# Scaled keys turned to token order by VectorE and SBUF transfers in place of TensorE, in a gated linear attention kernel followed by a feed-forward layer

## The chip, the core and the metric

The kernel runs as one program on one core of a Trainium2 chip. The metric is the device time of one execution in microseconds. The core's engines run side by side, each working through its own queue in order: TensorE (PE, with its weight loads shown apart as PEld), VectorE (DVE), ScalarE (ACT), GpSimd (POOL) and SyncE (SP), which here issues all transfers between device memory and the on-chip memory SBUF, and inside SBUF. Matmul results land in PSUM, which this kernel uses as eight banks.

## The reference

`state` is a 48 by 48 matrix for each of 4 batches and 8 heads. For each of 768 tokens it is decayed row by row by `alpha`, receives the outer product of `k` and `v`, and is read by `q`. The result, 3072 tokens by 384, goes through two matrix products with a leaky ReLU between them.

```python
for t in range(S):
    state = alpha[:, :, t, :, None] * state + np.einsum('bhd,bhe->bhde', k[:, :, t], v[:, :, t])
    y[:, :, t] = np.einsum('bhd,bhde->bhe', q[:, :, t], state)
...
h = x @ w_in
g = np.maximum(0.01 * h, h)
return (g @ w_out).astype(np.float32)
```

## The kernel before

The tokens are cut into 24 **units** of 128 tokens: unit u is token block u // 4 of batch u % 4, all 8 heads of it. Three units make one of eight **groups** of 384 tokens for the feed-forward layer.

The attention of a unit goes in eight steps (`attention`): `scans` (cumulative products of alpha, forward and backward), `scores` (keys times queries, line 356), `mask_scores`, `k_tokens`, `scaled_q`, `scaled_k`, `outputs` and `next_state`. The scans, `scaled_q` and `scaled_k` of unit u+1 stand between the steps of unit u. Keys and queries are scaled with the cumulative products in a layout with the head's 48 entries on the partitions and the tokens along the row (`ks`, `qs`: 128 partitions, 4 head pairs of 128 tokens each). `scores` uses that layout. The update of the state (line 412) needs the scaled keys the other way round, tokens on the partitions; `k_tokens` makes that: four TensorE transposes into a PSUM bank (line 380) and one ScalarE copy into SBUF (`ktok`, line 382). Units 20 to 23 are the last token blocks and update no state, so they skip it.

Alpha, q and k of units 0 to 8 are loaded token by token and turned by TensorE (line 280). From unit 9 on (`AHEAD`), they are loaded by four transfers each (line 146) in such a shape that one VectorE transpose in 32 by 32 blocks (line 289) gives the layout above. The transfers of these units write into fixed rooms in SBUF, two for each of alpha, q and k (`NL`), used in turn; units 0 to 8 have a third room each (`spare`). `load_next(u, i)` asks for the next load as soon as the room has been read.

The feed-forward layer is cut into **items** (i, f): group i, slice f of 16 of the hidden width. One item is 9 matmuls into a bank `ph` (line 493, two such banks), a ScalarE multiply and a VectorE maximum that free the bank (`t`, lines 496 and 499), a ScalarE rounding (`gh`, 501), a VectorE remainder (`gl`, 505), and, three items later in the code, 9 matmuls into the three output banks of the group (line 520). After 16 items, ScalarE copies the three outputs (`o`, line 532, two buffers) and SP sends them out (line 534). Groups 0 and 1 run alternately while the weights are converted; groups 2 to 7 run one after the other, and beside them the attention of units 9 to 23, one unit ahead of what the next group needs (`SL`, `LEAD`). `gather` (line 449) moves part of a group's attention output inside SBUF with two transfers before the group's first item.

The order of the instructions on each engine is not the order of the code: the tile framework schedules the whole program with its own estimate of times, and from there on the order is fixed. Groups 2 to 7 use three PSUM banks `a` for the attention in rotation (scores two, key transposes one, outputs one, state update one), three `b` for group outputs, two `ph`.

## Time and profile before

| | |
|---|---|
| median of 3 timed runs | 532.39 us (529.51 to 532.51) |
| span of the profiled execution | 530.9 us |
| TensorE busy, matmuls / weight loads | 518.5 us / 500.0 us |
| VectorE busy | 379.0 us |
| ScalarE busy | 230.7 us |
| GpSimd busy | 62.6 us |
| DMA queue of SP, share of 16 engines | 39.5% |

The profile gives the span from the first to the last instruction, not a separate time for that execution; the span lies between the lowest and the median of the timed runs. A line of a group of instructions reads: source line, engine, operation, output and inputs by name, count, then total busy time and the mean of one in nanoseconds, then the idle time of the engine just before them and who ended it. A line of the timeline reads: start and duration in us, engine, line, operation, names, count, and in brackets the idle time before it with what ended it. In the trace each single-precision matmul of lines 356, 395, 401 and 412 shows as two weight loads and two matmuls; the transposes of line 380 show as one each.

### The profile page before, as it was taken

The numbers are of one execution on the slowest core, as the hardware profiler recorded it, in microseconds if no ns is written. First come the engines' busy times: TensorE is split into PE (matmuls) and PEld (weight loads), VectorE is DVE, ScalarE is ACT, GpSimd is POOL, SyncE is SP. The second block draws the span as 40 slices with busy tenths as digits, with TensorE's granted clock in tenths as the row PEclk, the third lists the DMA queues.
The fourth block names the chain that finished last, engine by engine and source line by source line (L and its number), as shares of the span: only waits on it lengthen the run. The fifth ranks groups of instructions, "written<-read, shape, count | busy, mean of one in ns | idle before, by whom it ended". The sixth has DMA issues, their size and how long they took to land.

```text
span 530.9 us, 9962 instructions
## 1 busy us (share of the span) xinstructions
PE 518.5 (98%) x3778; PEld 500.0 (94%) x3778; DVE 379.0 (71%) x695; ACT 230.7 (43%) x489; POOL 62.6 (12%) x143
## 2 busy tenths in 40 slices
PE   8997999999999999999999999999999999999995
PEld 7886999999999999999999999999999999999995
DVE  6998899999999997777577586585786534333331
ACT  2764855555534444444334444345344444333331
POOL 4554500000000111100101101101010000000000
PEclk9998999999999999999999999999999999999998
DMA  9999975545726533552251431433201000101001
GB/s 144 168 175 170 229 172 133 131 122 141 170 45 184 127 84 81 102 134 49 60 111 30 112 83 44 92 74 86 54 15 25 31 16 1 23 1 44 1 0 51
DMA packets 92982, 46.64 MB, mean 88 GB/s; under 512 B 57856, under 2 KB 90112, under 8 KB 92928
## 3 DMA queue, kind: packets, MB, share of 16 engines
q1 hardware_dynamic: 92928, 45.93, 39.5%
q8 instruction: 32, 0.52, 0.4%
q14 instruction: 22, 0.18, 0.1%
HBM read 38.83 MB, written 4.72 MB: 82 GB/s over the span
## 4 chain that ended last, share of the span: by engine, by line
PE 87%; DVE 7%; DMA 4%; issue 1%; SPq 0%; DVEq 0%; ACT 0%
PE ph L493 35%; PE b L520 32%; PE a L356 4%; PE a L401 3%; PE a L520 3%; DMA small<-in_v_dram 3%; PE a L395 3%; PE a L412 2%; PE b L401 1%; PE a L380 1%; PE b L280 1%; DMA small<-in_alpha_dram 1%; DVE pw L262 1%; DVE gl L505 1%; DVE t L499 1%
## 5 line engine op out<-in xcount | busy, mean ns | idle before, releaser
L493 PE MATMUL ph<-large,w 128*128 128x384 f32 x1152 | 226.6, 338 | 0.5 <-DVE t L499 0.5
L493 PEld LDWEIGHTS ph<-large,w 128*128 128x128 f32 x1152 | 200.1, 188 | 2.8 <-DVE t L499 1.1
L520 PE MATMUL b<-w,gh 128*128 128x384 f32 x672 | 168.9, 340 | 0.0
L499 DVE TENSOR_TENSOR t<-ph,t 128x384 f32<-128x384 f32 x128 | 70.7, 553 | 79.1 <-ACT t L496 78.9
L520 PEld LDWEIGHTS b<-w,gh 128*128 128x128 f32 x672 | 119.4, 188 | 2.1 <-issue 0.4
L496 ACT ACTIVATE t<-ph 128x384 f32<-128x384 f32 x128 | 62.5, 489 | 128.2 <-PE ph L493 128.2
L501 ACT CAST gh<-t 128x384 fp32r<-128x384 f32 x128 | 65.7, 513 | 119.6 <-DVE t L499 119.6
L520 PE MATMUL b<-w,gl 128*128 128x384 f32 x336 | 107.4, 335 | 0.0
L505 DVE TENSOR_TENSOR gl<-t,gh 128x384 fp32r<-128x384 f32 x128 | 70.9, 554 | 34.3 <-ACT gh L501 34.2
L520 PEld LDWEIGHTS b<-w,gl 128*128 128x128 f32 x336 | 62.6, 188 | 0.0
L367 POOL TENSOR_SCALAR_AFFINE_SELECT sm<-sm 128x512 f32<-128x512 f32 x33 | 23.1, 712 | 207.8 <-ACT sm L366 207.8
L356 PEld LDWEIGHTS a<-qs,ks 48*128 48x128 f32 x312 | 24.1, 188 | 5.1 <-issue 4.2
L356 PE MATMUL a<-qs,ks 48*128 48x128 f32 x312 | 28.7, 285 | 0.0
L289 DVE STREAM_TRANSPOSE ks<-small 128x512 f32<-128x512 f32 x15 | 16.7, 1123 | 14.6 <-PE a L380 14.6
L324 POOL COPY pe<-pc 128x4 f32<-128x4 f32 x24 | 4.8, 202 | 163.7 <-DVE pc L314 163.7
L373 POOL TENSOR_TENSOR small<-us,pe 48x192 f32<-48x192 f32 x40 | 22.4, 560 | 1.5
L314 DVE TENSOR_TENSOR_SCAN pc<-e,small 128x128 f32<-128x128 f32 x60 | 20.4, 401 | 0.0
L366 ACT COPY sm<-a 128x512 f32<-128x512 f32 x24 | 14.0, 583 | 14.0 <-PE b L356 12.9
L520 PE MATMUL a<-w,gh 128*128 128x384 f32 x96 | 19.6, 337 | 0.0
L320 DVE TENSOR_TENSOR_SCAN rc<-e,small 128x511 f32<-128x511 f32 x15 | 19.1, 1276 | 0.2
L401 PE MATMUL a<-sm,small 128*48 128x128 f32 x256 | 17.7, 277 | 0.0
L254 ACT CAST w<-bits 128x768 fp32r<-128x768 f32 x16 | 13.4, 838 | 8.4 <-DVE bits L251 7.8
(92 smaller groups left out, 554.4 us busy)
## 6 DMA issues: line engine op xcount, KB each, us to landing
raw<-in_moe_w_out_dram SPq DMA_DIRECT2D x16, 384.0 KB, 3.8
small<-in_v_dram SPq DMA_DIRECT2D x24, 192.0 KB, 3.7
raw<-in_moe_w_in_dram SPq DMA_DIRECT2D x32, 144.0 KB, 4.0
out_dram<-o SPq DMA_DIRECT2D x24, 192.0 KB, 2.0
small<-in_alpha_dram SPq DMA_DIRECT2D x32, 96.0 KB, 2.3
small<-in_q_dram SPq DMA_DIRECT2D x30, 96.0 KB, 2.4
small<-in_k_dram SPq DMA_DIRECT2D x30, 96.0 KB, 2.2
small<-in_alpha_dram SPq DMA_DIRECT2D x30, 80.0 KB, 2.4
```

The lines of the kernel that those rows point to most:

```text
L314: nc.vector.tensor_tensor_scan(pc[:, p, :], aT[:, p, :], ones.broadcast_to([P, C]), 1.0, ALU.mult, ALU.mult)
L320: nc.vector.tensor_tensor_scan(flat[2][:, NP * C - 2::-1], flat[0][:, NP * C - 1:0:-1], flat[1][:, NP * C - 2::-1], last, ALU.mult, ALU.add)
L356: nc.tensor.matmul(ss[s][:, p, :], ks[lo:lo + D, p, :], qs[lo:lo + D, p, :], start=True, stop=True)
L367: made["mask", u] = nc.gpsimd.affine_select(out=sm[s], in_=sm[s], compare_op=ALU.is_ge, fill=0.0, base=0, pattern=[[0, NP], [1, C]], chann ...
L373: nc.gpsimd.tensor_tensor(*scalings.pop(0))
L401: nc.tensor.matmul(y[lo:lo + m, p, :], V[:, c:c + m], masked[u][s][:, p, :], start=not tb and p == 0, stop=p == NP - 1, skip_group_check=True,
L493: nc.tensor.matmul(ph, w_in_of(f, wn, g), xt[:, g, :], start=n == 0, stop=n == 3 * NG - 1)
L496: put(ordered, "ACT", lambda: nc.scalar.mul(t, ph, 0.01))
L499: put(ordered, "DVE", lambda: nc.vector.tensor_tensor(t, ph, t, ALU.max))
L501: put(ordered, "ACT", lambda: nc.scalar.copy(gh, t))
L505: made["gl", i, f] = put(ordered, "DVE", lambda: nc.vector.tensor_tensor(gl, t, gh.bitcast(F32), ALU.subtract))
L520: product = nc.tensor.matmul(po[j], gt[:, js], w_out_of(f, wn), start=f == 0 and n == 0, stop=f == NF - 1 and n == 2)
```

## The change

For units 9 to 19 the keys are no longer turned by TensorE and copied by ScalarE. After `scaled_k`, the new `turn_keys` lets VectorE transpose the scaled keys in 32 by 32 blocks (a second transpose for the unit, written into the room that the unit's k was loaded to), and 16 transfers inside SBUF, 32 partitions of 512 or 256 bytes each, put the blocks where they belong in the room that the unit's q was loaded to. The state update reads the keys from there. Within a token the four head pairs now alternate, so that the weights of one state-update matmul lie four elements apart. The next load of k waits until the 16 transfers have read, the next load of q until the state update has read. Alpha and k of units 9 to 23 have one room each in place of two; units 0 to 8 keep three. Units 0 to 8 keep the TensorE transposes.

```diff
--- before.py
+++ after.py
@@ -49,7 +49,8 @@
     ps_h = fast.enter_context(tc.tile_pool(name="ps_h", bufs=2, space=bass.MemoryType.PSUM))
     ps_x = fast.enter_context(tc.tile_pool(name="ps_x", bufs=3, space=bass.MemoryType.PSUM))
 
-    NL = 2, 2, 2
+    NL = 1, 2, 1
+    NS = 2, 1, 2
     NV = 3
     NBITS, NPW, NRAW = 2, 1, 4
     T4 = 4
@@ -89,7 +90,8 @@
     state, vals_sb, rest = rest[:B], rest[B:B + NV], rest[B + NV:]
     loads_sb = [[rest.pop(0) for _ in range(n)] for n in NL]
 
-    spare = pieces("spare", F32, *[(NP * PITCH,)] * 3)
+    spare = pieces("spare", F32, *[(NP * PITCH,)] * sum(NS))
+    spare_sb = [[spare.pop(0) for _ in range(n)] for n in NS]
     x_sb, = pieces("large", F32R, (3 * (NG + 1), 2, TB))
 
     w_sb = {}
@@ -110,7 +112,7 @@
         return tc.issue_after(made[key].ins) if key in made else nullcontext()
 
     def places(u, i):
-        return loads_sb[i] + [spare[i]] if u < AHEAD else loads_sb[i]
+        return loads_sb[i] + spare_sb[i] if u < AHEAD else loads_sb[i]
 
     def loaded(u, i):
         return places(u, i)[u % len(places(u, i))]
@@ -334,7 +336,8 @@
     def scaled_q(u):
         pc = live[u][0]
         qT = transposed(u, 1, "qs")
-        load_next(u, 1)
+        if not turns(u):
+            load_next(u, 1)
         qs = qT if u >= AHEAD else atp.tile([P, NP, C], F32, name="qs")
         nc.vector.tensor_tensor(qs, qT, pc, ALU.mult)
         live[u].append(qs)
@@ -342,10 +345,14 @@
     def scaled_k(u):
         pc, rc, pe, qs = live[u]
         kT = transposed(u, 2, "ks")
-        load_next(u, 2)
+        if not turns(u):
+            load_next(u, 2)
         ks = kT if u >= AHEAD else atp.tile([P, NP, C], F32, name="ks")
         made["ks", u] = nc.vector.tensor_tensor(ks, kT, rc, ALU.mult)
         live[u] = [pe, qs, ks]
+        if turns(u):
+            turn_keys(u, ks)
+            load_next(u, 2)
 
     def scores(u):
 
@@ -372,8 +379,30 @@
             while scalings:
                 nc.gpsimd.tensor_tensor(*scalings.pop(0))
 
+    turned = {}
+
+    def turns(u):
+        return u >= AHEAD and units[u][0] < NC - 1
+
+    def turn_keys(u, ks):
+
+        Q = 32
+        kq, ktok = (loaded(u, i)[:, 0:NP * C] for i in (2, 1))
+        nc.vector.transpose(
+            kq.rearrange("r (c e p) -> r p c e", c=C // Q, p=NP), ks.rearrange("r p (c t) -> r p c t", t=Q)
+        )
+        for r in range(0, P, Q):
+            n = min(Q, BR - r) * NP
+            for c in range(C // Q):
+                nc.sync.dma_start(
+                    ktok[c * Q:(c + 1) * Q, r * NP:r * NP + n], kq[r:r + Q, c * Q * NP:c * Q * NP + n]
+                )
+        turned[u] = ktok.rearrange("t (e p) -> t p e", p=NP)
+
     def k_tokens(u):
-        if units[u][0] < NC - 1:
+        if u in turned:
+            live[u][2] = turned.pop(u)
+        elif units[u][0] < NC - 1:
             ks = live[u][2]
             kt = bank()
             for p in range(NP):
@@ -413,6 +442,8 @@
                         kv[lo:lo + m, p, :], ktok[:, p, lo:lo + m], V[:, h * D:(h + 1) * D], start=True, stop=True
                     )
         load_values(u + NV)
+        if turns(u):
+            load_next(u, 1)
         live[u] = pe, kv
         xh, xl = (x_sb[0:BR, at:at + NP, n, j * C:(j + 1) * C] for n in (0, 1))
         made["xh", u] = nc.scalar.copy(xh, y[0:BR])
```

All line numbers above 52 shift. In the rows of the changed kernel below, 291 stands for 289 (VectorE transposes of loads), 316, 318 and 322 for 314, 316 and 320 (scans), 342 and 351 for 339 and 347 (scaling of q and k), 363 for 356, 371 for 364, 424 for 395, 430 for 401, 441 for 412, 450 for 419, 467 for 436, 524 for 493, 530 for 499, 536 for 505, 551 for 520; on SP 148 for 146 and 160 for 158. New are 391 (the VectorE transpose of scaled keys) and 397 (the 16 transfers).

**First place: TensorE where unit 9 begins**, in group 2. The names `w_801`, `w_1035` and so on are the weight slices of the items. Before:

```order
L493 MATMUL ph<-large,w_1017 128x384 x9
L520 MATMUL b<-w_801,gh 128x384 x5
L356 MATMUL a<-qs,ks 128x128 x8
L380 MATMUL a<-small,ks 128x112 x4
L493 MATMUL ph<-large,w_1035 128x384 x9
L520 MATMUL b<-w_801,gl 128x384 x2
L520 MATMUL b<-w_801,gh 128x384
L520 MATMUL b<-w_801,gl 128x384
L493 MATMUL ph<-large,w_1103 128x384 x7
L395 MATMUL a<-qs,small 112x128 x4
```

Now (`w_1254` is slice 7, `w_1329` slice 8, `w_1101` slice 5; before, `w_1017` was slice 3):

```order
L524 MATMUL ph<-large,w_1254 128x384 x6
L363 MATMUL a<-qs,ks 128x128 x8
L524 MATMUL ph<-large,w_1254 128x384 x2
L424 MATMUL a<-qs,small 112x128 x4
L524 MATMUL ph<-large,w_1254 128x384
L524 MATMUL ph<-large,w_1329 128x384 x9
L551 MATMUL b<-w_1101,gh 128x384 x2
L551 MATMUL b<-w_1101,gl 128x384
L441 MATMUL a<-small 64x48
L441 MATMUL a<-small 48x48
L441 MATMUL a<-small 64x48
L441 MATMUL a<-small 48x48
```

The four transposes of line 380 are gone. The scores of unit 9 have moved from behind slice 3 to inside slice 7, and the attention's matmuls, which stood in two blocks, stand in more and shorter ones, with feed-forward matmuls between them.

**Second place: the start of group 3.** TensorE before (`w_1616` and `w_1679` are slices 12 and 13 of group 2, `w_667` is slice 0 of group 3):

```order
L520 MATMUL b<-w_1616,gh 128x384 x2
L520 MATMUL b<-w_1616,gl 128x384
L493 MATMUL ph<-large,w_667 128x384 x9
L520 MATMUL b<-w_1679,gh 128x384 x2
L520 MATMUL b<-w_1679,gl 128x384
L520 MATMUL b<-w_1679,gh 128x384 x2
L520 MATMUL b<-w_1679,gl 128x384
L520 MATMUL b<-w_1679,gh 128x384 x2
L520 MATMUL b<-w_1679,gl 128x384
L395 MATMUL a<-qs,small 112x128 x4
L401 MATMUL a<-sm,small 48x128 x8
```

TensorE now (`w_1795` is slice 15 of group 2, `w_665` and `w_799` are slices 0 and 1 of group 3):

```order
L551 MATMUL b<-w_1795,gh 128x384 x2
L441 MATMUL a<-small 64x48
L551 MATMUL b<-w_1795,gl 128x384
L551 MATMUL b<-w_1795,gh 128x384 x2
L551 MATMUL b<-w_1795,gl 128x384
L551 MATMUL b<-w_1795,gh 128x384
L430 MATMUL a<-sm,small 48x128 x8
L551 MATMUL b<-w_1795,gh 128x384
L551 MATMUL b<-w_1795,gl 128x384
L524 MATMUL ph<-large,w_665 128x384 x9
L524 MATMUL ph<-large,w_799 128x384 x4
L441 MATMUL a<-small 48x48
```

Before, group 3 began while slices 13, 14 and 15 of group 2 still had their second products to come. Now all second products of group 2 stand ahead of it.

VectorE before, from the key transpose of unit 14 to slice 0 of group 3 (the second `t`) and on:

```order
L289 STREAM_TRANSPOSE ks<-small 128x4x4x32
L499 TENSOR_TENSOR t<-ph,t 128x384
L314 SCALAR_TENSOR_TENSOR pc<-e,small 128x128 x4
L315 MEMSET e 128x32
L316 RECIPROCAL small<-pc 128x32
L505 TENSOR_TENSOR gl<-t,gh 128x384
L320 SCALAR_TENSOR_TENSOR rc<-e,small 128x511
L499 TENSOR_TENSOR t<-ph,t 128x384
L347 TENSOR_TENSOR ks<-ks,rc 128x512
L289 STREAM_TRANSPOSE e<-small 128x4x4x32
L505 TENSOR_TENSOR gl<-t,gh 128x384
L289 STREAM_TRANSPOSE qs<-small 128x4x4x32
```

VectorE now, from the last step of unit 11's group (line 450) over the key transpose of unit 13 and slice 0 of group 3 (the first `t`) to slice 1 (the second `t`) and on:

```order
L450 TENSOR_TENSOR large<-a,large 112x4x128
L291 STREAM_TRANSPOSE ks<-small 128x4x4x32
L530 TENSOR_TENSOR t<-ph,t 128x384
L351 TENSOR_TENSOR ks<-ks,rc 128x512
L467 TENSOR_TENSOR us<-small,a 48x192 x2
L291 STREAM_TRANSPOSE qs<-small 128x4x4x32
L536 TENSOR_TENSOR gl<-t,gh 128x384
L391 STREAM_TRANSPOSE small<-ks 128x4x128
L530 TENSOR_TENSOR t<-ph,t 128x384
L342 TENSOR_TENSOR qs<-qs,pc 128x512
L291 STREAM_TRANSPOSE e<-small 128x4x4x32
L530 TENSOR_TENSOR t<-ph,t 128x384
```

Before, the key transpose of a unit stood more than one slice ahead of slice 0. Now that of unit 13 stands right ahead of slice 0's maximum, and the new transpose (line 391) ahead of slice 1's.

**Third place: SP's queue over one unit.** Before, the loads of k, alpha, q and v of one unit:

```order
L146 DMA small<-in_k_dram 32x4x192 x2
L146 DMA small<-in_k_dram 32x4x160 x2
L146 DMA small<-in_alpha_dram 32x4x192 x2
L146 DMA small<-in_alpha_dram 32x4x160 x2
L146 DMA small<-in_q_dram 32x4x192 x2
L146 DMA small<-in_q_dram 32x4x160 x2
L158 DMA small<-in_v_dram 128x8x48
```

Now, with the 16 transfers of unit 13 among them:

```order
L148 DMA small<-in_q_dram 32x4x192 x2
L148 DMA small<-in_q_dram 32x4x160
L397 DMA small<-small 32x128 x12
L397 DMA small<-small 32x64 x4
L148 DMA small<-in_k_dram 32x4x192 x2
L148 DMA small<-in_k_dram 32x4x160 x2
L148 DMA small<-in_q_dram 32x4x160
L565 DMA out_dram<-o 128x384
L148 DMA small<-in_alpha_dram 32x4x192 x2
L148 DMA small<-in_alpha_dram 32x4x160 x2
L160 DMA small<-in_v_dram 128x8x48
```

The 16 transfers stand behind most of the next load of q and ahead of the next loads of k and alpha. Before, no load of this stretch stood behind a transfer inside SBUF other than a gather.

## The prediction, made before the changed kernel was run

> **What bounds the kernel now.** I read the busy times and the chain of waits first, because they say which engine a saved microsecond must lie on:
>
> ```profile
> PE 518.5 (98%) x3778; PEld 500.0 (94%) x3778; DVE 379.0 (71%) x695; ACT 230.7 (43%) x489; POOL 62.6 (12%) x143
> ...
> PE 87%; DVE 7%; DMA 4%; issue 1%; SPq 0%; DVEq 0%; ACT 0%
> ```
>
> TensorE (PE) is busy for 98% of the span and makes 87% of the chain. Next I asked for busy times in two stretches of the stage in which units 9 to 19 run (columns: stretch, its length, then PE, PEld, DVE, ACT, POOL with counts, granted clock, DMA share, GB/s):
>
> ```profile
> 180.00:210.00 30.00, 30.00 (x215) 29.00 (x215) 24.80 (x48) 12.42 (x29) 4.23 (x10) 1.00 0.38 87
> 360.00:390.00 30.00, 30.00 (x219) 29.04 (x218) 20.82 (x40) 13.10 (x30) 4.11 (x10) 1.00 0.20 52
> ```
>
> PE is busy for all of both, at a granted clock of 1.00. VectorE has 5.2 us of 30 free in the first and 9.2 in the second. So in this stage time goes only with what PE has to issue, and comes only where PE is made to wait. Since a busy PE may hold several matmuls in flight, I price PE's work by the distance from one block's start to the next in the timeline (start, duration, idle before in brackets), not by durations. The pace of the units, from the scores of two units nine apart:
>
> ```profile
> 201.10 0.97 PEld L356 LDWEIGHTS a<-qs,ks 48*128 48x128 f32 x16 [0.25 <-issue]
> 383.22 0.97 PEld L356 LDWEIGHTS a<-qs,ks 48*128 48x128 f32 x16 [0.25 <-issue]
> ```
>
> 182.1 / 9 = 20.2 us a unit.
>
> **The transposes that go.** The groups of line 380 in the stage, and where the first and one other of them stand on PE:
>
> ```profile
> L380 PE MATMUL a<-small,ks x44: 257/258/314, 173.6 to 367.9; 112*128 112x112 f32 x44
> ...
> 172.51 0.97 PEld L356 LDWEIGHTS a<-qs,ks 48*128 48x128 f32 x16 [0.25 <-issue]
> 173.60 0.39 PEld L380 LDWEIGHTS a<-small,ks 112*128 112x128 f32 x4
> 173.94 1.51 PEld L493 LDWEIGHTS ph<-large,w 128*128 128x128 f32 x9
> ...
> 222.03 0.51 PEld L380 LDWEIGHTS a<-small,ks 112*128 112x128 f32 x4
> 222.50 0.30 PEld L520 LDWEIGHTS b<-w,gh 128*128 128x128 f32 x2
> ```
>
> 44 transposes, four a unit. The first four move what follows by 0.34 us (173.94 − 173.60), standing right behind the scores. The other ten sets stand alone, and each costs 0.47 (222.50 − 222.03). The two weight loads after it take 0.30 where such a pair elsewhere takes 0.36 (254.25, quoted below), so about 0.05 is given back. Sum: 10 × (0.47 − 0.05) + 0.34 = **4.5 us off PE**. One transpose lasts 258 ns, but four start within 0.47: they overlap, and 44 × 0.258 = 11.4 would count the same time twice. [...] ScalarE's copies of line 382 go with them; ScalarE is busy 12 to 13 us of 30 above, and no row has PE waiting for those copies: 0.
>
> **The new blocks.** The attention's single-precision matmuls stand between feed-forward ones, and each change between them costs something:
>
> ```profile
> 249.73 0.83 PEld L401 LDWEIGHTS a<-sm,small 128*48 128x48 f32 x16
> 250.53 0.59 PEld L412 LDWEIGHTS a<-small,ktok 128*64 128x64 f32 x16
> 251.18 0.30 PEld L520 LDWEIGHTS b<-w,gh 128*128 128x128 f32 x2
> ...
> 252.69 1.57 PEld L493 LDWEIGHTS ph<-large,w 128*128 128x128 f32 x9
> 254.25 0.36 PEld L520 LDWEIGHTS b<-w,gh 128*128 128x128 f32 x2
> ...
> 255.82 0.36 PEld L493 LDWEIGHTS ph<-large,w 128*128 128x128 f32 x2
> ...
> 414.24 1.01 PEld L395 LDWEIGHTS a<-qs,small 112*112 112x112 f32 x8
> 415.38 0.82 PEld L401 LDWEIGHTS a<-sm,small 128*48 128x48 f32 x16
> 416.39 1.52 PEld L493 LDWEIGHTS ph<-large,w 128*128 128x128 f32 x9 [0.18 <-PE a L401]
> 417.89 0.19 PEld L520 LDWEIGHTS b<-w,gh 128*128 128x128 f32 x1
> ```
>
> Line 401 followed by line 412 takes 0.80 to the next start; followed by the feed-forward layer it takes 1.01, and the nine loads behind that take 1.50 in place of 1.56. So one change costs 0.21 less 0.06, about 0.16 to the rounding of the rows. Behind line 412 it costs nothing that can be seen (0.65, then 0.30), and ahead of the scores 0.25 (201.10). In PE's order for units 9 to 19 I count 41 single-precision blocks before, ten of them transposes alone, and 47 now. That is 47 − 31 = 16 more, at 0 to 0.25 each: 0 to 4.0. I take the nearest row, 0.16: **+2.6**.
>
> **Weights four elements apart.** Line 412 (now 441) reads its weights with a step of 16 bytes. No matmul of before loads weights with a step, so I bound it. The 16 loads of a unit take 0.65 us to the next start (251.18 − 250.53), 0.041 each:
>
> ```profile
> L412 PEld LDWEIGHTS a<-small,ktok 128*64 128x64 f32 (+1 forms) x304 | 12.8, 134 | 0.7 <-ACT pc L332 0.5 <-issue 0.2
> ...
> L289 DVE STREAM_TRANSPOSE ks<-small 128x512 f32<-128x512 f32 x15 | 16.7, 1123 | 14.6 <-PE a L380 14.6
> ...
> L347 DVE TENSOR_TENSOR ks<-ks,rc 128x512 f32<-128x512 f32 x15 | 10.3, 686 | 0.0
> ```
>
> Lower end: 0, since one load lasts 134 ns while the next starts after 41, so a slower read may hide in the overlap. Upper end: a block that takes twice as long, 11 × 0.65 = 7.2. A gain is out, as the same numbers are read. The nearest row with a step is VectorE's transpose, which writes four elements apart and takes 1123 ns for 512 elements where a plain product takes 686; but it does another operation. The blocks are now shorter, one to four matmuls between feed-forward loads in several units, so some of the extra lies beside other work. I stay nearer the lower end: **+2.0**. [...]
>
> **VectorE.** The new transpose moves as many elements as that of line 289: 11 × 1.12 = 12.3 us. That is 1.1 in each 20.2 us, against 5.2 and 9.2 free in 30: it is covered by PE. If it stands right ahead of a `t` (line 499, which frees the bank that PE wants) the cover is thin. An old case of that:
>
> ```profile
> 161.09 2.04 DVE L289 STREAM_TRANSPOSE ks<-small 128x512 f32<-128x512 f32 x2
> 162.95 0.57 DVE L499 TENSOR_TENSOR t<-ph,t 128x384 f32<-128x384 f32 x1
> ...
> 163.57 1.53 PEld L493 LDWEIGHTS ph<-large,w 128*128 128x128 f32 x9 [0.79 <-DVE t L499]
> ```
>
> Two transposes ahead of `t` made PE idle for 0.79. In the new order the second no longer stands there: **−0.8**.
>
> **The transfers and the start of group 3.** Rows for what the new wait consists of:
>
> ```profile
> 263.74 1.74 SPq L146 DMA_DIRECT2D small<-in_k_dram  x4
> ...
> L449 SPq DMA_DIRECT2D large<-large x16: 568/584/1405, 39.1 to 451.8; - x16
> ...
> small<-in_k_dram SPq DMA_DIRECT2D x30, 80.0 KB, 2.3
> ...
> large<-large SPq DMA_DIRECT2D x16, 144.0 KB, 4.0
> ...
> L493 PE MATMUL ph<-large,w 128*128 128x384 f32 x1152 | 226.6, 338 | 0.5 <-DVE t L499 0.5
> ...
> L499 DVE TENSOR_TENSOR t<-ph,t 128x384 f32<-128x384 f32 x128 | 70.7, 553 | 79.1 <-ACT t L496 78.9
> ...
> L496 ACT ACTIVATE t<-ph 128x384 f32<-128x384 f32 x128 | 62.5, 489 | 128.2 <-PE ph L493 128.2
> ...
> L505 DVE TENSOR_TENSOR gl<-t,gh 128x384 fp32r<-128x384 f32 x128 | 70.9, 554 | 34.3 <-ACT gh L501 34.2
> ...
> L436 DVE TENSOR_TENSOR us<-small,a 48x192 f32<-48x192 f32 x22 | 7.6, 347 | 0.3
> ```
>
> SP's queue takes 0.435 us for one load of k (1.74 / 4) and 0.584 for a transfer inside SBUF of another shape; these land 2.3 and 4.0 us later. The 16 transfers so take 7.0 to 9.3 us to issue and 2.3 to 4.0 for the last to land. With one room, the last of the next four loads of k (0.43, landing 2.3; the others go out while the transfers land) waits for them, VectorE's key transpose (1.12) waits for that load, and everything behind it in VectorE's queue waits too. Where that transpose is ahead of a `t`, PE waits in the end.
>
> This decides at group 3. Slice 0's `t` there stands right behind the key transpose of unit 13. From the end of the first product of slice 13 of group 2, VectorE reaches the end of unit 12's new transpose after PE's tail 0.3 (0.338 for one matmul of line 493), `t` 0.49 + 0.55, key scaling 0.69, query transpose 1.10, two `us` 0.69, `gl` 0.55 and the transpose 1.12: 5.5 us. The chain from there to slice 0's `t` is issues, landing, 0.43 + 2.3 + 1.12 + 0.55: 13.7 to 17.7, middle 15.7. So slice 0's bank is free 19.2 to 23.2 us later. PE must have it for slice 2. Until then its order holds four first products and six second products at 1.57 (255.82 − 254.25), and the attention blocks (scores 1.09 + 0.25, line 395's 1.14, 401's 0.80, nearly two of 412's, 1.2): 20.2. It waits 1.0 (0 to 3.0). Slice 1's `t` stands behind the rest of unit 13 on VectorE: 0.69 + 0.69 + 1.12 + 0.55 + 1.12 + 0.55 = 4.7 later, while PE has 1.57 + 1.05 of work: 2.1 more. Second products would fill that, but all of group 2's have been issued ahead. **+3.1** (2.1 to 5.1, and 0 where the chain is faster than its lower end). At the later group starts second products of the old group still stand behind slice 0, as they did before: 0.
>
> **Sum.** −4.5 − 0.8 + 2.6 + 2.0 + 3.1 = +2.4. The profiled execution has a span of 530.9; the median of the runs is 532.4, 1.5 above it. 530.9 + 2.4 + 1.5 = **534.8**.
>
> **Rivals.** *Packed as before:* the transfers take less than the bounds, VectorE keeps ahead and the weights cost nothing. Left are −5.3 and 0.8 to 2.6 for the blocks: 527.9 to 529.7. For it: the windows, in which VectorE has room. Against it: the order at group 3.
>
> *The loop becomes the bound (slower):* new transpose, 16 transfers, load of k, key transpose and back to the new transpose, once a unit. At the upper ends: 9.3 + 4.0 + 0.43 + 2.3 + 1.12 + 4.15 (0.69 + 1.10 + 0.69 + 0.55 + 1.12) = 21.3, against a pace of 20.2 − 0.4 = 19.8. Ten loops lose 15; the state update is read about half a unit after the new transpose in the order, which takes some 9 less the landing of the transfers as reserve, so about 7 stays, and group 3 costs 5.1 in place of 3.1: 534.8 + 7 + 2 = 543.8. It decides from 11.8 us of issue and landing on (19.8 − 8.0); the middle of my bounds, 11.3, is close. Against it: at those middles the pace of 19.8 still holds, by 0.5.
>
> *Weights at the upper end:* 7.2 in place of 2.0: 540.0.
>
> **How the numbers follow.** Forecast 0.45 (531 to 539, by the bounds of blocks, weights and group 3); packed as before 0.25; the loop 0.20; the weights 0.10. A change of 1% (527.1, 537.7) is about the least that a measurement of this kernel can tell from none. Under 527.1 lie 0.06 of the packed case and 0.02 of the forecast. Above 537.7 lie 0.08 of the forecast, 0.19 of the loop and 0.08 of the weights: 0.35. Between them 0.57. The range from 527.0 to 546.0 leaves out about 0.08 below and 0.10 above, where the loop loses more than its reserve allows for.
>
> **What would show it.** PE's rows: no idle before the feed-forward products in groups 3 to 6 except near the start of group 3, where the idle is put down to `t`. The 16 transfers at 0.43 to 0.58 each on SP, the last landing within 4.0. Line 441 at 0.65 to 0.85 for 16 starts. I am wrong if PE idles at each unit behind the key transpose (the loop), if the weights of line 441 last far over 134 ns with PE full, or if the transfers take under 9 us in all and group 3 starts without a wait.

## The result, and the profile after

The changed kernel takes 545.74 us (median of 4 runs, 543.75 to 546.98) against 531.64 us (529.51 to 532.51): the ratio is 1.0262, 95% interval 1.0225 to 1.0299. It is slower, as forecast, but by 14 us where the forecast had 2.4. The time lies at the upper end of the range, 2 us above what the rival "the loop becomes the bound" gave (543.8).

The profiled execution took 543.75 us, the least of the four, and its span is 542.0 us, 11.1 more than before: the traces show 11 of the 14 us, and the rest lies between executions. Busy times and the chain of waits on the page of the changed kernel:

```profile
PE 523.1 (97%) x3734; PEld 498.7 (92%) x3734; DVE 390.9 (72%) x706; ACT 224.5 (41%) x478; POOL 71.9 (13%) x141
...
PE 65%; SPq 15%; DVE 8%; DMA 6%; issue 4%; ACT 1%; POOL 1%; DVEq 0%; ACTq 0%; POOLq 0%
```

VectorE has gained the 12 us of the new transposes. The new thing is in the chain: SP's queue, at 0% before, makes 15% of it, and TensorE has fallen from 87% to 65%. In stretches of 30 us (columns as in the prediction), TensorE is no longer full:

```profile
210.00:240.00 30.00, 27.32 (x195) 24.57 (x191) 19.29 (x35) 8.76 (x20) 2.55 (x5) 1.00 0.47 107
...
270.00:300.00 30.00, 27.85 (x212) 26.52 (x211) 22.22 (x39) 9.01 (x20) 2.97 (x5) 1.00 0.45 99
...
360.00:390.00 30.00, 28.15 (x215) 26.89 (x214) 22.28 (x42) 11.04 (x25) 4.42 (x7) 1.00 0.60 149
```

VectorE, with 8 to 11 us free in each, is not the engine that lacks time. The weight loads ahead of which TensorE stood idle longest in this stage, from the timeline (the idle time and what ended it in brackets):

```profile
235.60 1.53 PEld L524 LDWEIGHTS ph<-large,w 128*128 128x128 f32 x9 [1.86 <-DVE t L530]
...
295.33 1.51 PEld L524 LDWEIGHTS ph<-large,w 128*128 128x128 f32 x9 [2.38 <-issue]
...
357.77 1.35 PEld L524 LDWEIGHTS ph<-large,w 128*128 128x128 f32 x8 [1.21 <-DVE qs L342]
...
374.27 0.30 PEld L551 LDWEIGHTS b<-w,gh 128*128 128x128 f32 x2 [1.52 <-DVE t L530]
```

The first is the start of group 3; there 0.51 and 1.28 follow within 4.4 us, the three together 3.65. The others are at the starts of groups 4 and 5 and behind the latter, where 0.84 at 383.7 follows. What VectorE waits for is one line of the list of waits (total us, times, longest), and one unit of SP's and VectorE's timelines shows why:

```profile
DVE ks L291 <- DMA small<-in_k_dram: 26.8, 11, 3.9
```

```profile
219.74 10.38 SPq L397 DMA_DIRECT2D small<-small  x16
230.16 2.01 SPq L148 DMA_DIRECT2D small<-in_k_dram  x4
232.21 1.38 SPq L148 DMA_DIRECT2D small<-in_q_dram  x3
233.64 2.04 SPq L148 DMA_DIRECT2D small<-in_alpha_dram  x4
235.72 0.43 SPq L160 DMA_DIRECT2D small<-in_v_dram  x1
236.25 1.48 SPq L148 DMA_DIRECT2D small<-in_q_dram  x3
239.29 1.15 SPq L397 DMA_DIRECT2D small<-small  x2
```

```profile
234.08 1.08 DVE L291 STREAM_TRANSPOSE ks<-small 128x512 f32<-128x512 f32 x1 [3.39 <-DMA small<-in_k_dram]
...
238.19 1.08 DVE L391 STREAM_TRANSPOSE small<-ks 128x512 f32<-128x512 f32 x1
```

The 16 transfers of a unit hold SP for 10.38 us. The four loads of the next k go out behind them (230.16). The key transpose waits for the last of them and starts at 234.08, the new transpose follows 4.1 us later, and the next 16 transfers start 1.1 after that, at 239.29: a loop of 19.55 us. Over the ten loops of the stage the mean is 19.3 (first and last start of the new transpose, 161.6 and 354.8):

```profile
L391 DVE STREAM_TRANSPOSE small<-ks x11: 1051/1080/1096, 161.6 to 354.8; 128x512 f32<-128x512 f32 x11
```

In the unit shown SP issues for 17.7 of these 19.55 us (10.38 + 2.01 + 1.38 + 2.04 + 0.43 + 1.48).

The distances from start to start on TensorE, as in the prediction, summed over the stage from the first load that starts after 160 us to the end of the attention, in us (idle time counted apart, ahead of what it delays):

| | before | after | difference |
|---|---|---|---|
| key transposes | 5.0 | 0 | −5.0 |
| state updates (line 412, now 441) | 7.1 | 12.4 | +5.3 |
| idle ahead of feed-forward products | 1.5 | 11.4 | +9.9 |
| idle ahead of attention matmuls | 3.8 | 7.0 | +3.2 |
| all other matmuls | 272.2 | 269.6 | −2.6 |
| stage | 289.6 | 300.5 | +10.9 |

Of the −2.6, about 2.1 is no saving in this stage: it holds 12 feed-forward loads fewer now, at 0.17 us each, since the changed kernel is ahead when the stage begins. It starts the 33rd item of the feed-forward layer at 157.48 us, where the kernel before starts it at 159.63. From there to the last item it takes 13 us longer.

### The profile page after: what moved, and what is told of

Read it like the earlier page. It is cut to its first block, busy times and chain, and to the rows that moved or that the text cites. A ratio compares the mean times of both kernels' runs of the same rounds, so it can differ in the third digit from the quotient of the medians.

```text
span 542.0 us, 10205 instructions
## 1 busy us (share of the span) xinstructions
PE 523.1 (97%) x3734; PEld 498.7 (92%) x3734; DVE 390.9 (72%) x706; ACT 224.5 (41%) x478; POOL 71.9 (13%) x141
## 4 chain that ended last, share of the span: by engine, by line
PE 65%; SPq 15%; DVE 8%; DMA 6%; issue 4%; ACT 1%; POOL 1%; DVEq 0%; ACTq 0%; POOLq 0%
PE ph L524 26%; PE b L551 22%; SPq L397 11%; PE a L551 5%; SPq L148 4%; PE a L363 3%; PE a L430 2%; DMA small<-in_k_dram 2%; DMA small<-in_alpha_dram 1%; PE b L282 1%; PE a L424 1%; PE a L441 1%; DVE pc L316 1%; DMA raw<-in_moe_w_in_dram 1%; DVE rc L322 1%
## 5 line engine op out<-in xcount | busy, mean ns | idle before, releaser
L374 POOL TENSOR_SCALAR_AFFINE_SELECT sm<-sm 128x512 f32<-128x512 f32 x33 | 24.6, 759 | 139.7 <-ACT sm L373 139.6
L326 POOL COPY pe<-pc 128x4 f32<-128x4 f32 x24 | 6.3, 264 | 229.4 <-DVE pc L316 229.4
L291 DVE STREAM_TRANSPOSE ks<-small 128x512 f32<-128x512 f32 x15 | 16.6, 1104 | 26.8 <-DMA small<-in_k_dram 26.8
L380 POOL TENSOR_TENSOR small<-us,pe 48x192 f32<-48x192 f32 x40 | 24.5, 611 | 1.5
L322 DVE TENSOR_TENSOR_SCAN rc<-e,small 128x511 f32<-128x511 f32 x15 | 19.4, 1293 | 0.5
L373 ACT COPY sm<-a 128x512 f32<-128x512 f32 x24 | 14.0, 584 | 13.8 <-PE b L363 12.2
L430 PE MATMUL a<-sm,small 128*48 128x128 f32 x256 | 18.8, 278 | 0.2 <-POOL sm L374 0.2
L291 DVE STREAM_TRANSPOSE qs<-small 128x512 f32<-128x512 f32 x15 | 16.5, 1097 | 2.9 <-DMA small<-in_q_dram 2.7
```

Of the source, the lines that this page charges most:

```text
L291: nc.vector.transpose(t.rearrange("r p (j t) -> r p t j", t=T4), src.rearrange("r p (t d) -> r p t d", t=T4)[:, :, :, 0:32],)
L322: nc.vector.tensor_tensor_scan(flat[2][:, NP * C - 2::-1], flat[0][:, NP * C - 1:0:-1], flat[1][:, NP * C - 2::-1], last, ALU.mult, ALU.add)
L430: nc.tensor.matmul(y[lo:lo + m, p, :], V[:, c:c + m], masked[u][s][:, p, :], start=not tb and p == 0, stop=p == NP - 1, skip_group_check=True,
```

## The experiments

Ratios are to the kernel before on the same chip, with 95% intervals. Two questions came out of the table: what the stepped weights cost, and what the idle time comes from: the one room for k, which closes the loop, or SP's queue being full.

**1. The step alone, in the kernel before.**

```diff
-            ktok = atp.tile([P, NP, BR], F32, name="ktok", bufs=1)
-            made["sm", u] = nc.scalar.copy(ktok.rearrange("t p d -> t (p d)"), kt[:, 0:NP * BR])
+            ktok = atp.tile([P, BR, NP], F32, name="ktok", bufs=1).rearrange("t d p -> t p d")
+            made["sm", u] = nc.scalar.copy(ktok, kt[:, 0:NP * BR].rearrange("t (p d) -> t p d", p=NP))
```

> The kernel before, with its transposed keys laid out as in the changed kernel: the copy into ktok writes the four head pairs alternately, so that the state update's weights lie four elements apart, in all units. PE, VectorE and SP keep their order, row for row. Theory (a stepped weight read costs PE time): the weight loads of line 412 last about 190 ns in place of 134, a set of 16 takes about 1.05 us to the next start in place of 0.65, and the time goes up by 0.4 x 11 = 4.4 us in the stage, 1 to 3 more for units 0 to 8: +4 to +8 us. Rival (the longer loads lie beside other loads): the loads last 190 ns and the time stays within 1 us.

536.25 us, ratio 1.0090 (1.0075 to 1.0105): 5.3 us. The loads by form in this run and in the changed kernel:

```profile
L412 PEld LDWEIGHTS a<-small,ktok x304: 163/191/218, 14.1 to 380.1; 128*64 128x64 f32 x90, 128*48 128x48 f32 x62
```

```profile
L441 PEld LDWEIGHTS a<-small x176: 163/191/218, 185.7 to 387.3; 128*64 128x64 f32 x88, 128*48 128x48 f32 x88
```

The median load takes 191 ns where a contiguous one takes 129 (next experiment), and the state updates of the stage take 11.9 us start to start, 4.8 more. The edit also lengthens ScalarE's copy of line 382, from 533 to 980 ns, but TensorE's idle time stays the same (1.6 and 3.8 us against 1.5 and 3.8, last table). The longer load does not hide beside the next one: the theory held.

**2. Contiguous weights in the changed kernel.**

```diff
-            kq.rearrange("r (c e p) -> r p c e", c=C // Q, p=NP), ks.rearrange("r p (c t) -> r p c t", t=Q)
+            kq.rearrange("r (c p e) -> r p c e", c=C // Q, p=NP), ks.rearrange("r p (c t) -> r p c t", t=Q)
...
-                nc.sync.dma_start(
-                    ktok[c * Q:(c + 1) * Q, r * NP:r * NP + n], kq[r:r + Q, c * Q * NP:c * Q * NP + n]
-                )
+                nc.sync.dma_start(by_pair[c * Q:(c + 1) * Q, :, r:r + n], blocks[r:r + Q, c, :, 0:n])
```

> The changed kernel with the new transpose writing each head pair's 32 entries side by side and the 16 transfers placing them so that a matmul's weights are contiguous again (four runs of 128 bytes per partition in place of one of 512). PE's order is that of the changed kernel, row for row; VectorE and SP issue the same instructions in the same order. Theory (part of the loss is the stepped weight read): weight loads of the state update back at about 130 ns, 4 to 5 us faster than the changed kernel, 541. Rival (all of the loss is the wait of VectorE behind the transfers): no change, 545 to 546. If the smaller runs make the transfers land later by t, both go up by as much per stall.

546.02 us, ratio 1.0281 (1.0268 to 1.0295): no faster than the changed kernel, though the loads are short again:

```profile
L441 PEld LDWEIGHTS a<-small x176: 119/129/138, 185.3 to 387.4; 128*64 128x64 f32 x88, 128*48 128x48 f32 x88
...
DVE ks L291 <- DMA small<-in_k_dram: 31.6, 12, 4.5
```

The state updates take 7.6 us in place of 12.4, and the attention ends at the same time (460.6 us). New transposes still follow each other every 19.4 us (19.3 in the changed kernel), and the key transposes of units 10 to 20 all wait for their loads, as before this edit: the loop goes no faster. So the loss isn't a sum of parts. Of the 4.8 us that TensorE saved, 2.3 came back as idle time (0.4 and 1.9 in the last table), and 2.6 in all its other matmuls, of which some ran at a lower clock (0.64 from 295 to 299 us, told at the end). VectorE's wait for k has grown by 4.8 us too (31.6 from 26.8), but that is no sign of TensorE's saving: the edit spares VectorE 4.2 us of its own, since the new transpose no longer writes with a step and takes 701 ns in place of 1080. The transfers now consist of 128-byte runs; a transfer's median issue went from 588 to 599 ns and its landing from 1.8 to 1.9 us, which is too little to explain 4.8. What the time would be at the full clock, no run shows.

**3. Two rooms for k.**

```diff
-    NL = 1, 2, 1
-    NS = 2, 1, 2
+    NL = 1, 2, 2
+    NS = 2, 1, 1
```

> The changed kernel with two rooms for the later k loads in place of one, so that the next load of k needn't wait for the 16 transfers of the unit before; the framework orders it anew. Theory (the one room closes the loop of new transpose, transfers, load, key transpose): VectorE's 27 us of idle ahead of the key transposes fall to under 5, TensorE's idle ahead of feed-forward products falls from about 9 to 2 or less, and the time by 7 to 9 us, to 537 to 539. Rival (SP's queue is simply full of transfers, so that loads come late with any number of rooms): the wait for k stays over 15 us, and the time above 543.

540.34 us, ratio 1.0176 (1.0157 to 1.0195): 0.9% faster than the changed kernel, 4.7 us against each one's kernel before, where 7 to 9 were expected. VectorE's waits and the new transposes:

```profile
DVE qs L291 <- DMA small<-in_q_dram: 11.1, 7, 3.3
...
DVE ks L291 <- DMA small<-in_k_dram: 4.0, 5, 1.2
...
L391 DVE STREAM_TRANSPOSE small<-ks x11: 1081/1102/1128, 164.3 to 342.2; 128x512 f32<-128x512 f32 x11
```

The wait for k fell from 26.8 to 4.0 and the idle time ahead of feed-forward products from 11.4 to 3.2. The new transposes follow each other every 17.8 us on average, in place of 19.3. So the closed loop was the larger part of the stalls. But the wait for q rose from 2.7 to 11.1: SP's queue issues for 166 of the 180 us from 180 to 360 here (union of its rows in the timeline), 162 in the changed kernel and 66 in the kernel before. Opening the loop did not make the queue any emptier.

**4. The kernel before without the transposes.** Units 9 to 19 use the tokens of unit 8.

```diff
-        if units[u][0] < NC - 1:
+        if u >= AHEAD and units[u][0] < NC - 1:
+            live[u][2] = kept[-1]
+        elif units[u][0] < NC - 1:
```

> The kernel before without the transposes and copies of keys in units 9 to 19: their state updates read the tokens of unit 8 instead, so this part of the computation is left out. No new transpose, no transfers. It is the most that taking the transposes off PE can bring. Theory (44 transposes cost what their starts show, 4.5 us, and one stall of 0.8): 526 to 528. Rival (they cost their duration, 258 ns each, 11.4 us): 520.

527.63 us, ratio 0.9937 (0.9915 to 0.9958): 3.3 us. That is what the change could bring at most, with all that it adds free (in the order that the framework gave this run), and it is near the 4.5 of the starts and far from the 11.4 of the durations. The 0.8 us stall stayed.

**5. A quarter of the transfers.** One room for k as in the changed kernel.

```diff
-            for c in range(C // Q):
+            for c in range(0, C // Q, 4):
```

> The changed kernel with 4 of the 16 transfers of a unit (those of its first 32 tokens); the other 96 tokens of the keys stay unplaced, so this part of the computation is left out. One room for k as in the changed kernel, the new transpose and the stepped weights stay; the framework orders it anew. Theory (the queue's 10.4 us for 16 transfers close the loop): 2.6 us in their place, VectorE's wait for k loads falls from 26.8 to under 8, and the time to 536 to 539, as with two rooms or a little less. Rival (any transfer between transpose and load is enough, by its landing): wait over 15 and 543 or more.

537.88 us, ratio 1.0122 (1.0096 to 1.0148). VectorE's wait for k is 6.7 us, and SP issues for 95 of 180 us:

```profile
DVE qs L291 <- DMA small<-in_q_dram: 16.1, 10, 3.3
...
DVE ks L291 <- DMA small<-in_k_dram: 6.7, 4, 2.5
```

The room stayed, a landing still lies between the transposes, and yet the loop is no bound: it is the issuing of 16 transfers that closes it. 6.4 us were left over before (537.88 against 531.53 on that chip); the stepped weights account for 4.7 of these. What VectorE waits for most here is q, whose room is held until the state update has read it; that this room is the cause was not tested.

**6. The gathers on ScalarE's queue.** At the start of group 4 the changed kernel's TensorE waited 2.38 us (295.33 above); SP issues the gather that this group needs at

```profile
290.65 1.22 SPq L480 DMA_DIRECT2D large<-large  x2
```

behind 16 transfers and four loads of k, and its second transfer lands at 295.23. The records of the matmuls put the waits at the starts of groups 4 and 5 down to the gathers:

```profile
295.37 1.80 PE L524 MATMUL ph<-large,w 128*128 128x384 f32 x9 [2.15 <-DMA large<-large]
...
357.80 1.80 PE L524 MATMUL ph<-large,w 128*128 128x384 f32 x9 [0.92 <-DMA large<-large]
```

```diff
-            made["g", i] = nc.sync.dma_start(
+            made["g", i] = nc.scalar.dma_start(
```

> The changed kernel with the two gather transfers of each group (line 480) issued by ScalarE's queue in place of SP's; the framework orders parts of it anew. In the changed kernel the gathers of groups 4 and 5 stand on SP behind the 16 transfers, and TensorE waits 2.4 and 1.2 us at the starts of these groups. Theory (the gathers behind the transfers are a stall of their own, but the loop on k sets VectorE's pace): those two waits go, most of the gain comes back as wait elsewhere, 543 to 546. Rival (the stalls add up, each its own): 3.6 us faster, 542.

567.09 us, ratio 1.0675 (1.0655 to 1.0694). Both missed. No idle time over 0.6 us stands behind the gathers now (issued at 280.5 and 363.3 us), but the framework ordered parts of the kernel anew, and in the new order TensorE ran dry elsewhere. In the stage it stood 5.42, 2.34 and 1.95 us, the longest time where VectorE had waited 6.7 us for a load of k behind the transfers. About half of the loss lies earlier still: the first feed-forward product starts at 61.5 us in place of 50.8. ScalarE stands idle for 7.40 us around the issue of the first gather, with the copies of scores behind it in its queue, and TensorE for 7.11:

```profile
32.96 0.67 ACTq L480 DMA_DIRECT2D large<-large  x1
33.73 0.58 ACT L373 COPY sm<-a 128x512 f32<-128x512 f32 x1 [7.40 <-DMA raw<-in_moe_w_out_dram]
...
35.07 0.29 PEld L430 LDWEIGHTS b<-sm,small 128*64 128x64 f32 x2 [7.11 <-POOL sm L374]
```

Since so much of the order moved, the time says nothing certain of the gathers; that they stall the starts of groups 4 and 5 is read from the trace, and not shown by a run.

**7. Two rooms and contiguous weights.** The edits of 2 and 3 together.

> Two rooms for k and contiguous weights together. Theory (contiguous weights brought nothing with one room because the loop was the bound, and the loop is open with two): the weights now bring what they cost in the kernel before, 4.5 to 5.5 us off the 540.3 of two rooms alone: 535 to 536. Rival (the smaller runs of the transfers, 128 bytes in place of 512, cost as much as the contiguous weights bring): 540.

542.84 us, ratio 1.0220 (1.0197 to 1.0243), 2 us slower than with stepped weights (1.0176). The theory missed: opening the loop was not enough to let the contiguous weights pay. The state updates take 7.7 us in place of 12.7, and VectorE waits again:

```profile
DVE ks L291 <- DMA small<-in_k_dram: 10.0, 8, 2.7
DVE qs L291 <- DMA small<-in_q_dram: 10.0, 8, 2.3
...
DVE qs L291 <- DMA small<-small: 3.4, 1, 3.4
```

SP issues for 168 of 180 us. The instructions stand in the order of experiment 3. My new theory was that the full queue itself sets the pace, by the loop where there is one room and by late loads where there are two, and that whatever TensorE saves turns into waiting.

**8. and 9. Half of the transfers on ScalarE's queue.** With two rooms, once with contiguous weights (8) and once with stepped ones (9), which completes a set of four with 3 and 7:

```diff
-                nc.sync.dma_start(
+                (nc.sync if c < 2 else nc.scalar).dma_start(
```

> Two rooms for k, contiguous weights, and the 16 transfers of a unit shared by SP's and ScalarE's queues, 8 each; the framework orders it anew. It is the version that takes away each loss that has been found. What is left by the ledger: the transposes gone (-5), 3 to 4 us of new block changes on TensorE, little idle: 529 to 533 if ScalarE's 8 issues (about 4.7 us a unit) lie beside TensorE; 534 to 538 if they hold up its copies and multiplies.

> Two rooms for k and the transfers shared by SP's and ScalarE's queues, 8 each, with the weights stepped as in the changed kernel: the fourth of a set of four (SP's queue full or half empty, weights stepped or contiguous). With SP's queue full, contiguous weights brought nothing or less than nothing (545.7 to 546.0 with one room, 540.3 to 542.8 with two). Theory (SP's queue sets the pace where 16 transfers go through it, and hides what the weights cost; with 8, TensorE sets it): the price of the step comes back, 4.5 to 5.5 us over the 533.6 of the shared queues with contiguous weights: 538 to 539. Rival (the step's price is hidden in this arrangement of blocks, or the small runs of the transfers cost as much): within 1.5 us of 533.6.

| two rooms for k | weights stepped | weights contiguous |
|---|---|---|
| 16 transfers on SP | 1.0176 (1.0157 to 1.0195) | 1.0220 (1.0197 to 1.0243) |
| 8 on SP, 8 on ScalarE | 1.0178 (1.0153 to 1.0204) | 1.0037 (1.0024 to 1.0051) |

With half of the transfers elsewhere, the contiguous weights bring 1.4% (539.25 and 533.58 us, 8.7 and 2.1 above the kernel before on each one's chip); 4.6 us of that are the state updates themselves (11.9 and 7.3). With the queue full they bring nothing. So the theory held: the full queue hid the price of the step. The other way round, the step hides the price of the queue: with stepped weights the second queue brings nothing either (1.0176 and 1.0178). The two rows of the table also differ in the order that the framework gave them, the two runs of the lower row in a few places only. In 8 SP issues for 136 of 180 us, VectorE has no wait for k left that the list shows (8.4 us for q stay), and the idle time ahead of feed-forward products is 3.5 us. No wait of TensorE is put down to ScalarE's eight issues, though 14.2 us of wait of ScalarE's own multiplies and roundings are put down to these transfers. For transfers this small the issue is the longer part: 0.63 us from one issue to the next, 10.4 for the sixteen, against 1.8 to land, and sharing them between two engines was worth 9 us with contiguous weights (7 against 8).

**10. and 11. GpSimd's queue.** To beat the kernel before, something had to take the last 2 us away. With 8 transfers on SP and 8 on GpSimd (10), and with 4 on SP, 4 on ScalarE and 8 on GpSimd (11):

```diff
-                nc.sync.dma_start(
+                (nc.sync, nc.scalar, nc.gpsimd, nc.gpsimd)[c].dma_start(
```

> Two rooms for k, contiguous weights, 8 of the 16 transfers on SP's queue and 8 on GpSimd's, which is busy for 13% of the span; the framework orders it anew, with 43 single-precision blocks on TensorE over the whole kernel in place of the changed kernel's 54 and the 48 of before. Theory (what was left over before at 533.6 is block changes): 10 fewer at 0.16 to 0.25 take off 1.6 to 2.5, to 531. If GpSimd's issues are slow or hold up its masks and state scalings, which it does in order, TensorE waits for them at each unit: 536 to 545.

> Two rooms for k, contiguous weights, and the 16 transfers of a unit shared by three queues: 4 on SP, 4 on ScalarE, 8 on GpSimd; 45 single-precision blocks on TensorE over the whole kernel. With SP and GpSimd (8 and 8) the time was 533.2, with 5.6 us of idle ahead of feed-forward products, 2.1 and 1.4 of it behind VectorE's wait for loads of q and k. Theory (what is left over before is VectorE waiting for loads that stand behind transfers on SP): with 4 on SP this idle falls to about 2 and the time to 529 to 531. Rival (GpSimd's and ScalarE's issues take the place of the wait, in their own order): 532 to 536.

533.15 us, ratio 1.0047 (1.0030 to 1.0064), and 532.22 us, ratio 1.0015 (1.0006 to 1.0024). In 11 the transposes by VectorE lose no more than 0.2%, but no version is faster than the kernel before. Of the 3.3 us that experiment 4 puts as the limit, the new waits take most (4.2 us ahead of feed-forward products in 11, against 1.5).

**12. The rooms alone, in the kernel before.**

```diff
-    NL = 2, 2, 2
+    NL = 1, 2, 1
+    NS = 2, 1, 2
```

> The kernel before with one room for later alpha and k and two spare ones for the first units, as in the changed kernel, and the TensorE transposes kept; the framework orders it anew. Theory (rooms cost only where the transfers hold them): within 2 us of before, 530 to 533. Rival (one room alone makes the loads late): wait of VectorE for k and alpha over 10 us and 535 or more.

530.96 us, ratio 1.0013 (0.9995 to 1.0032). One room each costs nothing that can be measured as long as no transfer holds it.

The stage of each run in the same terms (us; the last column is when the attention ends in the profiled execution):

| | transposes | state updates | idle ahead of feed-forward | idle ahead of attention | attention ends |
|---|---|---|---|---|---|
| before | 5.0 | 7.1 | 1.5 | 3.8 | 449.7 |
| changed | 0 | 12.4 | 11.4 | 7.0 | 460.6 |
| 1 step alone | 5.0 | 11.9 | 1.6 | 3.8 | 453.3 |
| 2 contiguous | 0 | 7.6 | 11.8 | 8.9 | 460.6 |
| 3 two rooms | 0 | 12.7 | 3.2 | 9.0 | 458.0 |
| 4 no transposes | 0 | 7.2 | 1.6 | 4.5 | 445.0 |
| 5 a quarter | 0 | 11.8 | 1.8 | 7.4 | 454.7 |
| 6 gathers on ScalarE | 0 | 12.4 | 6.0 | 16.8 | 481.1 |
| 7 two rooms, contiguous | 0 | 7.7 | 6.2 | 11.6 | 459.3 |
| 8 two queues, contiguous | 0 | 7.3 | 3.5 | 7.1 | 448.7 |
| 9 two queues, stepped | 0 | 11.9 | 3.9 | 7.7 | 454.8 |
| 10 SP and GpSimd | 0 | 7.5 | 5.6 | 4.4 | 450.4 |
| 11 three queues | 0 | 7.3 | 4.2 | 5.0 | 448.3 |
| 12 rooms alone | 5.0 | 7.1 | 0.7 | 4.4 | 448.7 |

## Why the prediction was right or wrong

The direction was right, and most of the size was missed: +2.4 was forecast, and the trace shows +11.1. The forecast's own interval, 531 to 539, was missed too. The measured 545.74 lies 0.3 us inside a range that was made that wide for rivals held at 0.30 together, which is luck as far as the sum is concerned. Two of the three signs that the prediction named for being wrong came true at least in part: line 441's loads last 191 ns in place of 134 (16 starts take 1.1 us, not 0.65 to 0.85), and TensorE idles behind late key transposes, though not at each unit.

- *The transposes, −4.5.* Right: 5.0 us of starts are gone, and the run without them gained 3.3.
- *The stall of 0.8.* Right: no idle time over 0.4 us is left in the changed kernel between 150 and 235 us. It came back in several of the versions that were ordered anew, at about 0.9.
- *Sixteen more blocks, +2.6.* Right in size: the idle time ahead of attention matmuls rose by 3.2 us, 1.8 of it put down to issue. Where no single wait ahead of attention matmuls is over 0.4 us, it goes with the number of single-precision blocks in the stage: 4.4 us for 36 blocks (10), 5.0 for 38 (11), 7.1 for 46 (8), 7.0 for 47 (changed).
- *The stepped weights, +2.0 out of 0 to 7.2.* Mis-sized: 4.8 to 5.3. The step of the argument that failed is "a slower read may hide in the overlap" together with the shorter blocks. Starts 41 ns apart with loads of 134 were taken for room to spare; but where a load lasts half as long again (191), the starts lie about 70 ns apart (12.4 us for 176).
- *The start of group 3, +3.1.* Right: 3.65 us, in two pieces of 1.86 and 1.28 with 0.51 between, put down to `t` and `gl` as described. The parts came out differently: the transfers land in 1.8 us, not 2.3 to 4.0, but issue at 0.63 us from start to start, over the upper bound of 0.584; for the sixteen this is 2.2 us more than the middle of the bounds. Three of the next four loads of k go out while the last transfers land, as forecast, and the fourth behind them (the last transfer lands at 231.30, the loads go out at 230.16, 230.85, 231.26 and 231.86).
- *The later group starts, 0.* Wrong, and by itself the largest miss: some 6 us of idle lie there and behind (2.38, 1.21, 1.52, 0.84). I looked for the order of second products on TensorE alone, and not for what else stands behind the 16 transfers on SP. The gather of the next group does (290.65, and TensorE's matmuls wait 2.15 and 0.92 us for it at groups 4 and 5), and so does every load of k (11 waits of VectorE, up to 3.9 us).
- *Forecast against rival.* The loop was to decide from 11.8 us of issue and landing on, and the middle of my bounds was 11.3. Measured are 10.4 + 1.8 = 12.2, and it decided: the key transposes of units 10 to 20 all wait for their loads, and a second room or fewer transfers win time (3, 5). But the comparison behind the 11.8 was wrong. The whole loop takes 19.3 us on average, which is under the 19.8 that it was held against, so that by this condition it would not have decided. The 20.2 us a unit behind that figure is the mean of units 11 to 20 on TensorE; the scores of units 9 to 14 stand 17.0 us apart in the kernel before (172.51 to 257.64), and with two rooms the new transposes follow each other every 17.8. It is against such a pace that the loop is too long. So the rival's 543.8 came near the 545.74 in part by chance: it has 12.1 us of waiting ahead of feed-forward products (3.1 + 7 + 2) where the trace has 9.9 more than before, and 2.0 for the stepped weights where they cost some 5. That it held only 0.20 came from the issue price: I put the middle between a load's 0.435 and a gather's 0.584, when the row that is nearest to a transfer inside SBUF was the gather's.
- *What no step asked:* how full SP's queue gets. 16 × 0.63 + some 16 loads at 0.45 comes to 17 us in a unit of 20. With the loop open it is why the contiguous weights brought nothing (7) and 1.4% with half of the transfers elsewhere (8, 9).
- *Units 0 to 8, no term.* The changed kernel is 2.1 us ahead at the 33rd item (157.48 and 159.63). This hides a part of the loss: 13 us behind that point show as 11.1.

What stays open: what the changed kernel would take without the stalls at groups 4 and 5, what the order with the gathers on ScalarE's queue waited for in each of the 21 us that it lost more, and how much of the loss the clock takes in executions other than the profiled one.

## What to carry to other kernels

Add up the issue time of each queue per round before moving work to small transfers: sixteen at 0.63 us filled a queue that had been free for two thirds of the time, and the full queue set the pace with one room for k as with two (162 and 166 us of issue in 180). When what one engine saves does not show in the time, look for a second bound of the same size, and test two suspects together as well as alone: contiguous weights looked worthless until the queue was halved, and the second queue is worth nothing without them. Hold a loop against the pace of the units where it runs, not against their mean. An access that steps over 16 bytes is worth its own line in a sum: it lengthened TensorE's weight loads (129 to 191 ns), ScalarE's copy (533 to 980) and VectorE's transpose (701 to 1080).

## What the runs showed of the hardware that was not expected

In some runs a wait of TensorE cost more than its length. Where it stood idle for 2.4 us in the profiled execution of the changed kernel, its next nine loads took 1.51 us as ever. In the second and the sixth experiment it stood longer, by little in the one and by twice in the other, and came back at a lower clock, 0.64 and 0.50 in the windows below. Contiguous weights, the same place, and the window behind it (the granted clock is the third number from the end):

```profile
295.78 2.49 PEld L524 LDWEIGHTS ph<-large,w 128*128 128x128 f32 x9 [2.50 <-issue]
...
295.00:299.00 4.00, 3.19 (x13) 2.78 (x15) 3.79 (x6) 0.46 (x2) 0.00 (x0) 0.64 0.58 117
```

Gathers on ScalarE's queue:

```profile
270.87 1.81 PEld L363 LDWEIGHTS a<-qs,ks 48*128 48x128 f32 x16 [5.42 <-issue]
...
272.00:276.00 4.00, 4.00 (x22) 3.78 (x21) 3.45 (x8) 2.19 (x6) 2.43 (x5) 0.50 0.11 28
```

Nine loads take 2.49 us in place of 1.51 after a wait of 2.50, and sixteen take 1.81 in place of 0.97 after one of 5.42; the clock is back at 1.00 in the window from 280 to 284 us. In experiment 7 a wait of 2.44 us (to 229.20) was followed by a clock of 0.50 from 230.8 to 234.2. So waits of 2.44 and 2.50 us were followed by a lower clock. The one of 2.38 in the changed kernel was not (1.00 from 295 to 299 us) in the execution that the trace shows; in the other three the mean clock was lower, 0.985 to 0.997 against 0.999. Behind a wait of 2.34 us in experiment 6, five loads took 1.46 us in place of 0.88. No length from which on the clock falls can be read from these. This is a part of where the saving of experiment 2 went, and of the 567 us of experiment 6: in the stage, its feed-forward loads start 0.1750 us apart on average in place of 0.1722 before, which comes to some 4 us over 1355 of them, and a stretch at 0.50 from 31.3 to 41.5 us lies ahead of the stage.
